# Moving a router's logits and prefixes from TensorE transposes to VectorE transposes in blocks of 32

The chip is a Trainium2; the kernel runs on one core. The metric is the device time of one execution in microseconds (us), lower is better.

## The reference, cut to what matters

A short causal convolution over 8 x 3584 tokens of 192 channels, then a mixture of experts: each token takes the expert of its largest logit, or the one of the token before it when a local gate says so.

```python
# conv: 7 taps, one set of weights for each of 8 heads of 24 channels
out = np.einsum('hk,bskhg->bshg', w, x_unf)
# router and experts: E = 8, D = 192, F = 1024
logits = np.einsum('bsd,de->bse', x, w_gate)
local_gate = 1.0 / (1.0 + np.exp(-np.einsum('bsd,de->bse', x, w_local).squeeze(-1)))
for b in range(B):
    prev_e = -1
    for s in range(S):
        fresh_e = int(np.argmax(logits[b, s]))
        if s == 0 or local_gate[b, s] < 0.5:
            e = fresh_e
        else:
            e = prev_e if prev_e >= 0 else fresh_e
        prev_e = e
        p = ...                     # softmax of logits[b, s]
        h = np.maximum(x[b, s] @ w1[e], 0.0)
        out[b, s] = p[e] * (h @ w2[e])
```

## The kernel before

Tokens come in 16 groups of 128 x 14. For each group VectorE, ScalarE and (for groups 0 and 1) TensorE do the convolution; the router finds each token's expert and its slot; GpSimd scatters the rows to their slots in DRAM; 144 expert blocks gather rows, multiply and scatter the results. The first 35 blocks hold one unit of 128 tokens, the next 87 two, the last 22 one. The router's logits need tokens' channels on partitions, so TensorE transposes them first:

```python
for u in range(3):                                   # three sets of 16 transposes
    tps = [hps_p.tile([P, 4 * GQ, DR], F32, name="hps") for half in range(2)]
    ...
                turn_half(tps[half][:, GQ * j + q, :], src, half)
    ...                                              # ScalarE evicts
lps = hps_p.tile([P, 2 * P], F32, name="hps")
for u in range(3):
    for j in range(4):                               # 12 products, 32 columns wide
        nc.tensor.matmul(lps[32 * j:32 * j + 32, :w], lhsT=wg[:, u, :],
                         rhs=yT[:, u, j, :w], start=(u == 0), stop=(u == 2))
# ... four transposes back; later two transposes for the carry, one back,
nc.tensor.matmul(nps[:, :E], lhsT=tri, rhs=mine, start=True, stop=True)    # prefix
nc.tensor.matmul(nps[:, E:2 * E], lhsT=ones, rhs=mine, start=True, stop=True)
```

The main loop deals out this work in steps between the products; `put()` issues one scatter of 128 routed rows:

```python
for i, (_, n, _, _) in enumerate(blocks):
    ensure(i)
    weights(i + AHEAD)
    hT = hidden(n, wbs[i], xT)
    if i + 1 < len(blocks):
        xT = turn(blocks[i + 1][1], xgs[i + 1])
    step(2.1 * n, 1)                      # conv and router work, then one put()
    output(n, wbs.pop(i), xgs.pop(i), hT)
    step(2.1 * n, n)                      # the same, then n put()
```

## Time and profile before

| | us |
|---|---|
| timed runs before the change (3) | 1482.4 to 1483.17, median 1482.96 |
| span of the execution that was profiled | 1412.9 |
| of which until block 0 / one-unit blocks / two-unit blocks / last 22 | 71.8 / 220.4 / 993.1 / 127.5 |

The stages run from the start of a block's first hidden product to that of a later one. Where TensorE does nothing but blocks, a two-unit block takes 10.81 us, so 87 would take 940.5. The first two lines don't agree by 70 us (68 by the profiled execution's own time, 1414.58).

### The profile page before, as it was taken

To read this page: it belongs to the slowest core of one execution; us is meant where nothing else is said; L and a number is where in the kernel's file an instruction comes from. 1 tells how busy PE (TensorE), PEld (TensorE's weight loads), DVE (VectorE), ACT (ScalarE), POOL (GpSimd) and SP (SyncE) were. 2 spreads that over 40 slices of the span, in tenths; PEclk is the share of its full clock that TensorE was granted. 3 is DMA by queue.
4 is the path that set the end of the run, shared out by engine and by line. 5 is a ranking of instruction groups with operands and counts; after the bars stand their busy time and mean duration, and the time that the engine had idled before them with its cause. 6 is when DMAs were issued, how large, how long until landed. Compare 5 with 4: busy or idle time off the path is not lost.

```text
span 1412.9 us, 41146 instructions
## 1 busy us (share of the span) xinstructions
PE 1377.8 (98%) x17132; PEld 1292.3 (91%) x17132; DVE 754.4 (53%) x1947; ACT 488.0 (35%) x1168; POOL 495.5 (35%) x524
## 2 busy tenths in 40 slices
PE   6788999999999999999999999999999999999998
PEld 4488999999999999999999999999999999999998
DVE  6767878777777777777777776241111111111111
ACT  3234344343333433334333343322222222222332
POOL 1342345344343443444434344344212111211111
PEclk9899999999999999999999999999999999999999
DMA  4399989977575775757757556566555555557893
GB/s 173 103 397 361 329 335 415 363 278 296 184 282 201 262 262 203 268 202 263 263 202 268 202 207 209 200 222 238 203 175 200 204 178 179 204 186 247 314 327 136
DMA packets 66476, 343.99 MB, mean 243 GB/s; under 512 B 12656, under 2 KB 23655, under 8 KB 45810
## 3 DMA queue, kind: packets, MB, share of 16 engines
q1 hardware_dynamic: 44064, 288.66, 56.6%
q0 software_dynamic: 22224, 52.70, 9.7%
q8 instruction: 135, 2.21, 0.6%
q14 instruction: 51, 0.42, 0.1%
q10 hardware_dynamic: 2, 0.00, 0.0%
HBM read 288.51 MB, written 53.49 MB: 242 GB/s over the span
## 4 chain that ended last, share of the span: by engine, by line
PE 62%; issue 27%; POOL 6%; DMA 3%; ACT 1%; DVE 1%; POOLq 0%; SPq 0%; ACTq 0%
PE yps L660 26%; PE hps L645 26%; POOL out_dram L674 5%; PE xps L264 2%; PE hps L264 2%; PE hps L308 2%; POOL slots L467 1%; DMA wb<-in_w_dram 1%; PE yps L185 1%; PE hps L185 1%; DMA xg<-slots 1%; DMA x_sb<-in_x_dram 1%; DMA out_dram<-o_sb,xg 0%; DVE y_sb L202 0%; PE hps L407 0%
## 5 line engine op out<-in xcount | busy, mean ns | idle before, releaser
L645 PE MATMUL hps<-xT,wb 64*128 64x256 f32 (+1 forms) x6912 | 635.1, 337 | 1.7 <-DMA wb<-in_w_dram 1.0
L660 PE MATMUL yps<-wb,hT 64*128 64x192 f32 x7392 | 635.8, 325 | 0.0
L645 PEld LDWEIGHTS hps<-xT,wb 64*128 64x128 f32 x6912 | 568.8, 188 | 45.3 <-DVE o_sb L670 5.4
L660 PEld LDWEIGHTS yps<-wb,hT 64*128 64x128 f32 x7392 | 601.1, 188 | 1.1 <-issue 0.9
L674 POOL DMA_INDIRECT out_dram<-o_sb,xg x231 | 236.9, 1025 | 772.4 <-DVE o_sb L670 681.7
L202 DVE SCALAR_TENSOR_TENSOR y_sb<-x_sb,c,y_sb 128x336 f32<-128x336 f32 x720 | 412.6, 583 | 22.3 <-ACT y_sb L177 6.6
L650 ACT ACTIVATE hT<-hps 128x512 f32<-128x512 f32 (+1 forms) x576 | 263.9, 510 | 379.9 <-PE hps L645 379.9
L467 POOL DMA_INDIRECT slots<-y_sb,posi x224 | 219.6, 980 | 115.4 <-issue 107.5
L669 ACT ACTIVATE o_sb<-yps,xg 128x192 f32<-128x192 f32 x231 | 87.6, 418 | 482.7 <-PE yps L660 482.7
L670 DVE SCALAR_TENSOR_TENSOR o_sb<-yps,xg,o_sb 128x192 f32<-128x192 f32 x231 | 88.3, 414 | 293.5 <-ACT o_sb L669 278.2
L625 DVE COPY xT<-xps 128x768 f32<-128x768 f32 x87 | 83.3, 957 | 236.1 <-PE xps L264 236.1
L264 PEld LDWEIGHTS xps<-ident,xg 64*128 64x128 f32 x1386 | 66.4, 140 | 13.6 <-issue 4.5
L264 PE MATMUL xps<-ident,xg 64*128 64x64 f32 x1386 | 67.8, 222 | 5.6 <-DMA xg<-slots 5.6
L628 DVE COPY xT<-xps 128x384 f32<-128x384 f32 x57 | 31.6, 555 | 70.4 <-PE xps L264 70.3
L177 ACT ACTIVATE y_sb<-x_sb,c 128x336 f32<-128x336 f32 x116 | 67.0, 589 | 0.4
L301 ACT COPY yT<-hps 128x512 f32<-128x512 f32 x93 | 49.8, 598 | 2.6 <-PE hps L264 2.2
L308 PE MATMUL hps<-yT,wg 128*32 128x256 f32 (+1 forms) x384 | 24.5, 358 | 2.7 <-issue 2.4
L264 PE MATMUL hps<-ident,y_sb 64*128 64x64 f32 x512 | 21.1, 223 | 2.8 <-DVE y_sb L202 1.7
L264 PEld LDWEIGHTS hps<-ident,y_sb 64*128 64x128 f32 x512 | 19.8, 139 | 4.2 <-ACT y_sb L177 1.8
L185 PE MATMUL hps<-x_sb,wb 128*128 128x336 f32 x56 | 18.7, 502 | 4.1 <-DMA x_sb<-in_x_dram 4.1
L308 PEld LDWEIGHTS hps<-yT,wg 128*32 128x32 f32 x384 | 11.9, 109 | 10.8 <-issue 5.7
L185 PEld LDWEIGHTS hps<-x_sb,wb 128*128 128x128 f32 x56 | 12.0, 217 | 10.5 <-issue 6.1
(142 smaller groups left out, 369.0 us busy)
## 6 DMA issues: line engine op xcount, KB each, us to landing
wb<-in_w_dram SPq DMA_DIRECT2D x144, 1536.0 KB
x_sb<-in_x_dram SPq DMA_DIRECT2D x16, 1920.0 KB
xg<-slots SPq DMA_DIRECT2D x87, 258.0 KB
xg<-slots SPq DMA_DIRECT2D x57, 129.0 KB
out_dram<-o_sb,xg POOLq DMA_INDIRECT x231
slots<-y_sb,posi POOLq DMA_INDIRECT x224
slots<-pad SPq DMA_DIRECT2D x1, 129.0 KB
slots<-pad,toi POOLq DMA_INDIRECT x8
```

The lines of the kernel that those rows point to most:

```text
L177: nc.scalar.activation(cols(h), chans(h, 0), Act.Copy, scale=c[:, h, 0:1])
L202: nc.vector.scalar_tensor_tensor(cols(h), chans(h, k), c[:, h, k:k + 1], cols(h), Alu.mult, Alu.add)
L264: nc.tensor.transpose(to, src[rows], identity=ident[rows, rows])
L308: nc.tensor.matmul(lps[32 * j:32 * j + 32, :w], lhsT=wg[:, u, :], rhs=yT[:, u, j, :w], start=(u == 0), stop=(u == 2))
L467: ins = nc.gpsimd.indirect_dma_start(out=slots[:, :], in_=rows, in_offset=None, out_offset=bass.IndirectOffsetOnAxis(ap=to, axis=0)).ins
L625: nc.vector.tensor_copy(to.rearrange("p h d k s -> p h (d k) s"), at.rearrange("p h d k s -> p h (d k) s"))
L645: nc.tensor.matmul(hps[half][:, j, w], lhsT=wb[rows, f0:f0 + P], rhs=xT[rows, d, w], start=(d == 0 and j == 0), stop=(d == KD - 1), skip_g ...
L650: nc.scalar.activation(hT[:, m:m + 2, w], hps[half][:, :, w], Act.Relu)
L660: nc.tensor.matmul(yps[half][:, k * D:(k + 1) * D], lhsT=hT[rows, m, k * P:(k + 1) * P], rhs=wb[rows, WA + m * D:WA + (m + 1) * D], start= ...
L669: nc.scalar.activation(o_sb[:, k, :], y[0], Act.Copy, scale=gate)
L670: nc.vector.scalar_tensor_tensor(o_sb[:, k, :], y[1], gate, o_sb[:, k, :], Alu.mult, Alu.add)
L674: sent = nc.gpsimd.indirect_dma_start(out=out, in_=o_sb[:, k, :], in_offset=None, out_offset=bass.IndirectOffsetOnAxis(ap=xg.bitcast(I32)[ ...
```

## The change

VectorE transposes the tokens where they lie, in blocks of 32 x 32 within a partition group of 32. The logits are then 48 small products (64 rows, 32 columns of weights, 128 tokens) in one visit to TensorE, eight side by side in the array. Carry and prefix over partitions go through VectorE's transposes and scans, not through TensorE. Groups 0 and 1 keep the old path. The diff, cut to its core (where weights are loaded and how the router's are laid out is left out):

```diff
+    def logits(g, y_sb):
+        ...
+        for t in range(0, NT, TQ):                        # TQ = 4 of 14 columns
+            nc.vector.transpose(z[:, t:u, :], y_sb[:, t:u, Y0:Y0 + D])
+        yield "hop"
+        lps = [hps_p.tile([P, TQ * Q], F32, name="hps") for half in range(2)]
+        begin = [min(TQ * j, NT - TQ) for j in range(4)]
+        for b in range(DQ):                               # DQ = 6 blocks of 32 channels
+            for j in range(4):
+                for half, rows in halves():
+                    nc.tensor.matmul(lps[half][Q * j:Q * j + Q, :], lhsT=wgq[rows, b, :],
+                                     rhs=z[rows, begin[j]:begin[j] + TQ, b * Q:(b + 1) * Q],
+                                     start=(b == 0), stop=(b == DQ - 1))
+        ...            # two ScalarE copies, a transpose back, 16 VectorE copies of 32 partitions
-        rps = hps_p.tile([P, GQ * P], F32, name="hps")
-        nc.tensor.transpose(rps[:1, :P], run[:, NT - 1:NT], identity=ident)
-        nc.tensor.transpose(rps[:1, P:2 * P], keep, identity=ident)
+            nc.vector.transpose(rT..., rk...)             # carry: 2 transposes, 10 small copies
-        nc.tensor.matmul(nps[:, :E], lhsT=tri, rhs=mine, start=True, stop=True)
-        nc.tensor.matmul(nps[:, E:2 * E], lhsT=ones, rhs=mine, start=True, stop=True)
+            nc.vector.transpose(mT, mk)                   # prefix: 2 transposes, 2 scans, 8 copies
-        step(2.1 * n, 1)
+        step(2.5 if n == 1 else 4.2, 1)
-        step(2.1 * n, n)
+        step(2.5 if n == 1 else 4.2, n)
```

## The prediction

> **What bounds the kernel now.** I read the page first, then the stretches by engine, the chain that ended last in order of time, and the timelines of TensorE and VectorE. The page's busy line:
>
> ```profile
> PE 1377.8 (98%) x17132; PEld 1292.3 (91%) x17132; DVE 754.4 (53%) x1947; ACT 488.0 (35%) x1168; POOL 495.5 (35%) x524
> ```
>
> TensorE is busy throughout, but an average hides stages, so I cut the span. Columns: stretch, length, busy time of PE, PEld, DVE, ACT, POOL with counts, granted clock, DMA share, GB/s.
>
> ```profile
> 125.00:180.00 55.00, 55.00 (x875) 53.35 (x874) 42.45 (x117) 23.59 (x67) 17.10 (x17) 1.00 0.95 357
> 410.00:470.00 60.00, 60.00 (x731) 55.23 (x729) 44.86 (x115) 23.26 (x54) 26.15 (x26) 1.00 0.67 242
> 925.00:1290.00 365.00, 365.00 (x4214) 353.25 (x4212) 63.99 (x145) 97.82 (x204) 85.10 (x88) 1.00 0.56 195
> ```
>
> There are three stages. From about 72 to 292 us the expert blocks hold one unit of 128 tokens, and TensorE, DMA (0.95) and VectorE are all nearly full. From 292 to about 925 us blocks hold two units; TensorE alone is full, VectorE at 75%, while conv and router of groups 5 to 15 run beside. After 925 us no routing is left. The routing groups are 2 to 15; groups 0 and 1 are routed in the prologue, on a path that the change keeps. What the router costs TensorE is seen in the chain of the middle stage (start, length, piece):
>
> ```profile
> 351.61 0.50 PE hps L264 x16
> 357.71 0.50 PE hps L264 x16
> 358.22 5.25 PE yps L660 x64
> 363.47 1.43 PE hps L308 x15
> 364.90 5.38 PE hps L645 x48
> 376.03 0.20 PE hps L362
> 376.23 0.11 PE hps L363
> 382.09 0.15 PE hps L376
> 387.64 0.32 PE hps L407 x2
> 387.96 0.22 PE hps L408 x2
> 399.19 5.18 PE hps L645 x44
> ...
> 417.10 2.98 PE yps L660 x35
> ```
>
> The reader is to see that the router's pieces stand between blocks of hidden (L645) and output (L660) products with no gap: each is time on the path. One group repeats after 417.10 - 358.22 = 58.88 us and holds five blocks. A block without routing is read from the timeline of TensorE after 925 us:
>
> ```profile
> 1010.15 5.43 PE L660 MATMUL yps<-wb,hT 64*128 64x192 f32 x64
> 1020.95 5.43 PE L660 MATMUL yps<-wb,hT 64*128 64x192 f32 x64
> ```
>
> 10.80 us, so five are 54.0, and a group's routing costs 4.9 us of TensorE. By pieces: three sets of 16 transposes 1.5, logits 1.43, four transposes back 0.12, carry 0.31 + 0.15, prefix 0.54, together 4.05; the other 0.8 is in the pieces that follow an interruption (5.38 against 5.18).
>
> In the first stage it is VectorE that I distrust. Its timeline over one conv-only block:
>
> ```profile
> 168.75 0.55 DVE L628 COPY xT<-xps 128x384 f32<-128x384 f32 x1
> 169.22 2.37 DVE L202 SCALAR_TENSOR_TENSOR y_sb<-x_sb,c,y_sb 128x336 f32<-128x336 f32 x4
> 171.65 0.42 DVE L670 SCALAR_TENSOR_TENSOR o_sb<-yps,xg,o_sb 128x192 f32<-128x192 f32 x1
> 171.98 2.26 DVE L202 SCALAR_TENSOR_TENSOR y_sb<-x_sb,c,y_sb 128x336 f32<-128x336 f32 x4
> 174.17 0.55 DVE L628 COPY xT<-xps 128x384 f32<-128x384 f32 x1
> ```
>
> Eight taps (about 0.58 us each) and two evictions take 5.42 us without a gap, and TensorE's one-unit block takes 5.52. VectorE is already even with TensorE here.
>
> **What the Trainium skill says.** "TensorE: Matmul & The Clock Gate", Part 3: products of at most 64 rows or 32 columns run side by side in different tiles, each further tile starting some 4 ns later. The trace agrees on columns: the 12 logits products (9 of 256 columns, 3 of 128, 2688 in all) took 1.43 us; at the 0.437 us per lone 256-column product (24 hidden products, two abreast, in 5.24) they would take 4.6, so over three ran at once. "TensorEngine Tiling (Array Packing)", Key Properties: changing the tiling mode drains the array; the 0.2 us after a visit fits. "Vector Engine (DVE) Microarchitecture Reference", 3.8: the 32x32 transpose sustains one element per cycle per lane; no such operation is in this trace. "VectorE: DVE Perf Modes", Two Vector instructions with no wait between them: an instruction whose start quadrant differs from the last one's waits for all earlier ones. The small copies added here go from quadrant to quadrant; the trace before has none such.
>
> **The change, part by part.** I compared the built programs. For 14 groups TensorE loses 48 + 4 transposes, 12 wide logits products, two carry transposes, one back and two prefix products; it gains 48 products of 64 rows x 32 columns x 128 tokens, in one visit.
> - The visit: 24 one-unit hidden products of 128 columns, two abreast, take 2.68 us, 0.223 a round. Eight abreast, 48 products are 6 rounds: 1.34 us, with a start and the slower piece after it some 1.7. If issue limits instead, the closest measured rate is 16 transposes in 0.50 us, 31 ns for a load and a product; 48 products are 96 such pairs (two records each): 3.0, with its surroundings 3.2. I take 1.9, nearer the first, because four tiles abreast are shown and eight are not.
> - Gain on the path in the middle stage: 4.9 - 1.9 = 3.0 a group. Eleven groups: 33 us.
> - VectorE gains per group 2688 transposed columns in four pieces (an estimate of 0.96 GHz by the skill's clock: 2.8 + 0.3), one of 256 columns (0.35), four small ones, and some 34 small copies. Copies of this size take 0.13 to 0.17 here; overlapped they add 0.09, held 0.16. Sum 8 to 10 us. ScalarE loses six evictions of 0.60, two of lsb, two of lt and three small ones, and gains two copies of 0.25: off the path.
> - In the middle stage the built order gives six blocks a group, not five, with 55 to 57 us of VectorE in 6 x 10.8 + 1.9 = 66.7 us. It fits. Routing ends some ten blocks later, still ahead of need.
> - In the first stage the budget per step goes from 2.1 to 2.5: conv-only blocks hold ten taps, 0.47 + 0.33 + 10 x 0.58 = 6.6 us, over TensorE's 5.52. Adding VectorE's pieces over blocks 1 to 34 in the built order gives 202 to 209 us, against 173 before; TensorE needs 34 x 5.52 + 3 x 1.9 = 193, and the stage took 220 before with its DMA waits. The three groups' TensorE gain (9 us) is thus mostly taken back by VectorE: I count 0, from -8 to +8.
> - Prologue: a shorter copy, five more memsets, a larger weight load: under 1 us. After 925 us: nothing.
>
> Sum: 33 us off. The profiled run took 1414.58, the timed ones 1483; I cannot explain the 68 us from this trace and take the saving as it is: 1450.
>
> **The rivals.**
> (a) The visit is limited by issue, not streaming. For: nothing here shows pairs closer than 31 ns. Against: those transposes load 128 columns each, and loads of 32 should be shorter (L308's mean load is 109 ns, the transposes' 139). It would leave 1.7 a group: 19 us, 1464, within 2%.
> (b) VectorE becomes the bound of the first stage and costs more than TensorE gains. For: the 6.6 us blocks. Against: the lighter blocks between (4.8 to 5.7) and some 2 us of slack from the output products let it average. At worst 10 us lost: 1460.
> (c) The logits visit waits for VectorE's transposes, a new wait in place of those removed. Against: the order puts the visit a step after them, and hidden plus output products give 5 us of slack in the middle stage. If it happened, 1 us a group: 1461.
> (d) All router TensorE time was hidden anyway. The chain contradicts it: it ran through these pieces, and the period was 4.9 longer than the same blocks without.
>
> **Range and chances.** Streaming (60%) gives 34 to 39 off, issue-bound 19 to 25; the first stage adds 8 either way; if the timed runs are slower all through, the gain grows by 5%. That spans 1434 to 1466. The 2% line is 29.7 us off, 1453.3: a little above my centre. Faster by over 2%: 0.6; within 2%: 0.38; slower: 0.02.
>
> **What would show it.** Right: the logits visit takes 1.4 to 1.9 us in the chain; two-unit groups repeat every 66 to 67 us with six blocks; VectorE's busy time grows by about 110 to 140 us; the first two-unit block starts within 8 us of 292. Wrong: a visit near 3 us (rival a); the chain of the first stage running through VectorE with the stage longer than 220 us (b); TensorE idle just before the visit, released by VectorE (c).

## The result, and the profile after

1476.59 us median (1474.74 to 1480.2, 4 runs) against 1482.77 (1482.4 to 1483.17, 4 runs): ratio 0.9961, 95% interval 0.9942 to 0.998, so within 2%. A ratio here is the mean time of one kernel's fast runs over that of the other's of the same rounds, so not quite the ratio of the medians quoted. A time is compared only with one of the same chip.

The busy line of the page after (busy us, share of the span, instructions):

```profile
PE 1393.4 (94%) x17314; PEld 1315.6 (89%) x17314; DVE 896.7 (61%) x2605; ACT 434.6 (29%) x1014; POOL 479.3 (33%) x515
```

TensorE is at 94%, where the profile before had 98%: it has become idle in places, and VectorE has grown by 142 us, just over the 110 to 140 foreseen. The chain in order of time through one logits visit (start, length, piece):

```profile
529.09 0.59 PE hps L350 x31
529.67 0.17 issue
...
531.73 0.32 issue
532.04 1.07 PE hps L350 x50
533.11 5.40 PE yps L756 x64
```

L350 is the line of the 48 products (96 records). The visit takes 533.11 - 529.09 = 4.0 us instead of the predicted 1.9. Its first 31 records and its last 50 run at about 20 ns each; between them TensorE stands still several times, and the profile calls that "issue": it waited for nothing that is recorded. Such stops stand in the output products too. So the first question was whether the profile before, which has hardly any, is of a usual execution.

### The profile page after: what moved, and what is told of

It reads as the page before. It is cut to its first block, busy times and chain, and to the rows that moved or that the text cites. A ratio compares the mean times of both kernels' runs of the same rounds, so it can differ in the third digit from the quotient of the medians.

```text
span 1474.5 us, 41949 instructions
## 1 busy us (share of the span) xinstructions
PE 1393.4 (94%) x17314; PEld 1315.6 (89%) x17314; DVE 896.7 (61%) x2605; ACT 434.6 (29%) x1014; POOL 479.3 (33%) x515
## 4 chain that ended last, share of the span: by engine, by line
PE 58%; issue 23%; DVE 8%; POOL 5%; DMA 2%; another core or an unknown queue 2%; ACT 1%; POOLq 0%; DVEq 0%; SPq 0%; ACTq 0%
PE yps L756 26%; PE hps L741 24%; POOL out_dram L770 4%; DVE y_sb L206 3%; PE hps L350 3%; PE xps L278 2%; POOL slots L566 1%; PE yps L189 1%; PE hps L189 1%; DMA wb<-in_w_dram 1%; DVE xT L727 1%; DVE o_sb L766 1%; DMA out_dram<-o_sb,xg 1%; DMA x_sb<-in_x_dram 0%
## 5 line engine op out<-in xcount | busy, mean ns | idle before, releaser
L756 PE MATMUL yps<-wb,hT 64*128 64x192 f32 x7392 | 672.4, 327 | 23.2 <-issue 19.1
L756 PEld LDWEIGHTS yps<-wb,hT 64*128 64x128 f32 x7392 | 615.3, 188 | 48.4 <-issue 42.7
L741 PEld LDWEIGHTS hps<-xT,wb 64*128 64x128 f32 x6912 | 608.6, 188 | 21.8 <-DVE xT L727 9.5
L206 DVE SCALAR_TENSOR_TENSOR y_sb<-x_sb,c,y_sb 128x336 f32<-128x336 f32 x720 | 402.9, 568 | 20.3 <-ACT y_sb L181 2.5
L278 PEld LDWEIGHTS xps<-ident,xg 64*128 64x128 f32 x1386 | 78.0, 140 | 3.4 <-PE hps L741 0.3
L278 PE MATMUL xps<-ident,xg 64*128 64x64 f32 x1386 | 77.0, 223 | 0.1
L350 PE MATMUL hps<-z,wg 64*32 64x128 f32 x1344 | 44.7, 286 | 16.0 <-issue 15.7
L350 PEld LDWEIGHTS hps<-z,wg 64*32 64x32 f32 x1344 | 25.5, 110 | 32.0 <-issue 31.1
L366 DVE COPY lt<-lq 32x36 f32<-32x36 f32 x224 | 44.6, 199 | 3.3
L340 DVE STREAM_TRANSPOSE z<-y_sb 128x768 f32<-128x768 f32 (+1 forms) x56 | 44.1, 844 | 0.0
```

Source lines behind the costliest of these rows:

```text
L206: nc.vector.scalar_tensor_tensor(cols(h), chans(h, k), c[:, h, k:k + 1], cols(h), Alu.mult, Alu.add)
L278: nc.tensor.transpose(to, src[rows], identity=ident[rows, rows])
L350: nc.tensor.matmul(lps[half][Q * j:Q * j + Q, :], lhsT=wgq[rows, b, :], rhs=z[rows, begin[j]:begin[j] + TQ, b * Q:(b + 1) * Q], start=(b = ...
L741: nc.tensor.matmul(hps[half][:, j, w], lhsT=wb[rows, f0:f0 + P], rhs=xT[rows, d, w], start=(d == 0 and j == 0), stop=(d == KD - 1), skip_g ...
L756: nc.tensor.matmul(yps[half][:, k * D:(k + 1) * D], lhsT=hT[rows, m, k * P:(k + 1) * P], rhs=wb[rows, WA + m * D:WA + (m + 1) * D], start= ...
```

## The experiments

"Gap" below means: two weight loads of TensorE start over 0.4 us apart, counted in the trace of the two-unit stage from 330 to 1340 us, from start to start. So it holds the usual step from load to load too (0.08 us in output products, 64 in 5.4), and sums of gaps are somewhat more than the time lost.

### The kernel before again, the budget, and the size of the visit (chip 5)

`e1_before` is the kernel before, unchanged.

> The kernel before, unchanged, for a new profile: its timed runs are 1483 us, but the profile on which the prediction rests was of an execution of 1414.6, while the changed kernel's profile (1476.3) agrees with its timed runs. Theory U (the profile of before was of a lucky execution; the timed ones lose some 68 us in a way it does not show): the new profile is near 1481 us, with gaps of TensorE that are put down to issue, as the changed kernel's profile shows them. Rival (the profiler itself makes this kernel faster): the profile is again near 1413 us with no such gaps, the timed runs near 1483. Time against before: 1.00.

Measured: 1481.88 us, ratio 0.9997 (0.998 to 1.0013); profiled span 1483.9. From its page, and its view of what TensorE waited for (us in total, times, longest):

```profile
PE 1416.5 (95%) x17132; PEld 1326.4 (89%) x17132; DVE 742.9 (50%) x1947; ACT 493.8 (33%) x1168; POOL 493.8 (33%) x524
PE yps L660 <- issue: 15.1, 34, 1.1
```

The same program at 95% of 1483.9 us, not 98% of 1412.9: on this chip it has the gaps as well, 60 us of them in the two-unit stage, where the first profile had 18. Theory U held: that profile was of another kind of execution than the timed runs.

`e2_budget` gives the steps of the changed kernel back their old budget.

```diff
-        step(2.5 if n == 1 else 4.2, 1)
+        step(2.1 * n, 1)
-        step(2.5 if n == 1 else 4.2, n)
+        step(2.1 * n, n)
```

> The changed kernel with the old step budget (2.1 per one-unit step instead of 2.5). Theory V (VectorE is the bound of the first stage because conv-only blocks hold ten taps): the first two-unit block starts earlier than the 321 us of the changed kernel, near 300, and the time falls by 10 to 25 us, to about 1455. Rival S (TensorE's instruction supply costs the time, stage by stage, whatever VectorE does): the first stage shortens by less than 5 us and the time is within 0.5% of the changed kernel's 1476.

Measured: 1488.15 us, 1.0048 (1.0029 to 1.0068). Its one-unit stage is shorter (217.1 us against 240.4) and its two-unit stage longer (1057.2 against 1025.5): less routing is done early and more late. The first two-unit block does start at 297.7 us, as theory V said, but the time rises by 12 us instead of falling; S, which had the first stage almost unchanged, missed too. The new budget isn't what ate the gain.

`e3_half` uses two column tiles of 224 columns, so 24 products instead of 48; `e4_few` does only the first 8 of the 48, with a wrong result.

```diff
-TQ = (NT + 3) // 4                  # e3_half
+TQ = (NT + 1) // 2
-            for j in range(4):
+            for j in range(2):
-        for b in range(DQ):         # e4_few
+        for b in range(1):
```

> The logits visit of the changed kernel as 24 products of 7 tokens x 32 instead of 48 of 4 x 32: two column tiles instead of four, four abreast instead of eight. Half the instructions (48 load and product pairs instead of 96), longer streaming: 6 rounds x 224 columns, an estimate of 2.3 us from the 0.223 us a round of 128 columns takes. Theory S (the visit is limited by the supply of instructions to TensorE: in the changed kernel's profile it takes 4.0 us with gaps of 0.3 us after every 4 or 5 records): the visit falls from 4.0 to 2.4 to 3.0 us, and the time by 11 x 1 to 1.5 = 11 to 17 us, to about 1462. Rival (streaming or the tile-mode switch limits the visit): it gets longer, 4.5 us or more, and the time rises by 5 us or more. Eight copies and two long transposes on VectorE instead of sixteen and four also take 1.6 us a group off VectorE.

> Wrong result on purpose: the logits visit does only the first 8 of its 48 products; all else is as in the changed kernel (the numbers of blocks do not depend on the routing). It measures what the visit costs in all. Theory S: the gaps put down to issue in and near the visits go with the 40 products, a group repeats some 4 us sooner, and the time falls by 14 x 3 to 4 = 42 to 56 us, to about 1425. Rival (the gaps are not the visit's; they come at every so many instructions anyway): the visit's 4 us go but gaps appear in the products that follow, and the time falls by less than 25 us.

Measured: 1455.16 us, 0.9816 (0.9799 to 0.9833), and 1433.0, 0.9666 (0.965 to 0.9682). Fewer products in the visit do gain. The visits of `e3_half` in the two-unit stage take 3.1 to 3.8 us, above theory S's 2.4 to 3.0 and below its rival's 4.5, and the time fell further than S said. `e4_few` gains 44 us on the changed kernel, inside S's 42 to 56. But with 8 products left there are still 52 us of gaps, mostly inside output products, so the visit is not their only place.

### The parts alone, and work added at the end (chip 1)

After the last group is routed some 25 two-unit blocks run undisturbed; `f1_busy` and `f2_visits` add one suspected cost there. `pa_logits` has the new logits with the old carry and prefix on TensorE, `pb_prefix` the reverse.

```diff
         # pa_logits: carry and prefix as before, by transposes and products of TensorE
-        if alone:                       # carry
+        if not alone:
+            rps = hps_p.tile([P, 2 * P], F32, name="hps")
+            nc.tensor.transpose(rps[:1, :P], run[:, NT - 1:NT], identity=ident)
         ...
-        if alone:                       # prefix: TensorE's branch for all groups
+        if True:
         # pb_prefix
-        lt = yield from (wide_logits if alone else logits)(g, y_sb)
+        lt = yield from wide_logits(g, y_sb, alone)
         # f1_busy, each step of a two-unit block at the end
+        for _ in range(6):
+            nc.vector.scalar_tensor_tensor(toy[:, 0, :], toy[:, 1, :], c[:, 0, 0:1],
+                                           toy[:, 0, :], Alu.mult, Alu.add)
+        ...                                  # two ScalarE copies, one GpSimd copy
         # f2_visits, every sixth step there: the 48 products on a constant tile
```

> The new logits alone (VectorE transposes, one visit), with carry and prefix through TensorE as in the kernel before. Theory S (the visit is held up by TensorE's supply of instructions, about 4.0 us where the old pieces took 1.5 + 1.43 + 0.12 = 3.05): this part gains nothing, about 1.0 us a group lost for 11 to 14 groups, less what the longer group period saves; about 1487 us, from 1479 to 1495, visit 3.6 to 6 us in the chain. Rival (the visit is well paid for, and the gain of the change comes from it): 1476 or less.

> The new carry and prefix on VectorE alone, with the old transposes and wide logits products on TensorE. It takes five short pieces, 0.31 + 0.15 + 0.54 = 1.0 us a group, from TensorE and adds no burst. Theory S: this part carries the gain, 11 to 16 us: about 1469 us (1464 to 1475), faster than the whole change. Rival (the visit carries it): 1480 or more.

> The changed kernel; after the last group is routed, each of the two steps of a two-unit block adds idle work of about the size that conv and router have: six VectorE operations of 128x336, two ScalarE copies, one GpSimd copy, with nothing that waits for them. TensorE's program and all transfers stay. Rival O (TensorE's gaps in the middle stage come of the other engines' work, which delays what its products wait for): the undisturbed blocks grow from 10.81 us to 11.3 to 11.6, some 25 of them, 1488 to 1497 us. Theory S: they stay at 10.81, time as the changed kernel, 1475 to 1479.

> The changed kernel; after the last group is routed, every third two-unit block gets a further visit of 48 of the same products on a constant tile, with no conv, router or VectorE work beside it. Theory S: the visit is slow by itself where it meets the edge of a fetched piece of the program, 2.5 to 4.5 us each as in the middle stage, and the blocks around it show gaps too: some 8 visits, +24 to +36 us, about 1505. Rival O: without other work beside it a visit takes its streaming time with a restart, 1.4 to 1.7 us, and no gaps appear: +12 to +15 us, about 1490.

Measured: 1405.6, 1397.46, 1381.9 and 1395.64 us. The kernel before stood at 1412.95 (1412.04 to 1416.15, 7 runs), not at 1482: this chip gives the time of the first profile. The ratios are 0.994 (0.9923 to 0.9956), 0.9886 (0.987 to 0.9903), 0.978 (0.9763 to 0.9796) and 0.9871 (0.9854 to 0.9887). The absolute times expected were worked out for 1482 and don't apply, and nor does a test of gaps where there are none. What stands: both parts gain, 7.3 and 15.5 us (in the two-unit stage 18.6 and 19.7; the one-unit stage of `pa_logits` is 10 us longer, 230.7); the idle work of `f1_busy` costs nothing, its blocks staying at 10.81 us; and eight visits added in `f2_visits` cost 1.7 us each (13.4 us of records for them in the groups of its profile).

`g1_after` is the changed kernel unaltered, `g2_half` the same as `e3_half`, both on chip 1.

> The changed kernel itself, unaltered, to be read with the time of the kernel before in the same call, because the last call stood at 1413 us for the kernel before where the earlier ones stood at 1482. Theory C (the prediction's steps hold where TensorE gets its instructions in time, and the gain is lost only where it doesn't): if the kernel before stands near 1413, the changed one takes 1376 to 1384, ratio 0.974 to 0.980, visit 1.6 to 1.75 us; if it stands near 1482, about 1476 again, ratio 0.994 to 0.998. Rival (the idle work of f1_busy and the added visits of f2_visits changed something else, and the changed kernel gains little anywhere): ratio above 0.985 in both.

> The visit with two column tiles of 224 columns instead of four of 128: 24 products instead of 48, the same as e3_half. Theory C: near 1413 for the kernel before, the visit takes 24 products at two tiles of rows by two of columns, four abreast, 6 rounds of 224 columns: 6 x 0.39 = 2.3 us with its restart, 0.6 to 0.7 more than the 1.7 of four column tiles, so 7 to 10 us more than the changed kernel: 1384 to 1392. Near 1482 for the kernel before: 1455 again. So the better form would hang on the supply. Rival: it is faster than the changed kernel in both, as fewer instructions are better anywhere.

Measured: 1381.6 us (1380.91 to 1382.89), ratio 0.9774 (0.9758 to 0.979), and 1389.45, 0.983 (0.9813 to 0.9846). What theory C said of a chip of 1413 came true in all of it; what it said of one of 1482, and its reason, were not tested here. The busy line and the chain of `g1_after`:

```profile
PE 1342.8 (97%) x17314; PEld 1273.7 (92%) x17314; DVE 896.5 (65%) x2605; ACT 434.2 (31%) x1014; POOL 484.5 (35%) x515
```

```profile
554.15 1.67 PE hps L350 x94
555.82 5.40 PE yps L756 x64
...
620.81 1.72 PE hps L350 x94
```

The visit takes 1.7 us without a stop, and the next one comes 66.66 us later, six blocks of 10.81 and the visit. Here the change gains 31 us. With 24 products the visit takes 2.40 us (six rounds of 224 columns instead of 128), and is the slower form.

### Whether it is the visit or other engines' work (chips 12, 10)

`h1_phases` puts three stretches into the end of one kernel: visits, plain blocks, and idle work of other engines. `h2_third` uses three column tiles of 160 columns, 36 products.

```diff
+            steps[0] += 1                    # h1_phases, after the last group is routed
+            if steps[0] <= 16:
+                if steps[0] % 4 == 0:
+                    visit()
+            elif steps[0] > 32:
+                busy()
-TQ = (NT + 3) // 4                           # h2_third
+TQ = (NT + 2) // 3
```

> The changed kernel; after the last group is routed, the two-unit blocks come in three stretches: eight with a visit of 48 products in every second one, eight as they are, the rest with idle VectorE, ScalarE and GpSimd work of the size of conv and router. It is for a chip on which the kernel before takes about 1482 us; on one of 1413 it only repeats what f1_busy and f2_visits showed (about 1389 us, visits 1.65 us, no gaps). At 1482: theory V (a visit alone runs TensorE's supply dry) has the four visits at 2.5 to 4.5 us with gaps in the outputs near them, and the last stretch at 10.81 us a block. Theory O (all engines draw on one slow supply, so TensorE starves only where the others fetch too) has visits of 1.6 to 2 us, no gaps in the first two stretches, and 11.3 to 11.6 us a block in the last one.

> Three column tiles of 160 columns: 36 products where the change has 48 and the half form 24, six abreast. Per round 160 columns at the rate of the half form (2.40 us for 6 rounds of 224 columns, 0.40 a round): 6 x 0.286 = 1.7 us, the same as the visit of 48 (1.70), so with 24 fewer of its 96 pairs at no loss. At 1413 for the kernel before: 1381 to 1384, ratio 0.976 to 0.980. At 1482: between the change (1476) and the half form (1455), about 1465.

Measured on chip 12, where the kernel before took 1413.24: 1390.85 us (2 runs) and 1381.69, 0.9779 (0.9762 to 0.9795). A visit of 36 products takes 1.78 us, so its fewer records are no gain and no loss there. The four added visits of `h1_phases` take 1.83, 1.84, 1.83 and 1.52 us; the difference is taken up below. To get to a slow chip both were sent again, unaltered, as `h3_phases` and `h4_third`.

> The same kernel as h1_phases, sent again in the hope of a chip on which the kernel before takes about 1482 us, where alone it can tell the theories apart. There, theory V (a visit alone runs TensorE's supply dry): four visits of 2.5 to 4.5 us with gaps in the outputs near them, the last stretch at 10.81 us a block. Theory O (all engines draw on one slow supply): visits of 1.6 to 2 us, no gaps in the first two stretches, 11.3 to 11.6 us a block in the last. On a chip of 1413 it repeats h1_phases, 1389 to 1393 us, and tells nothing new.

> The same kernel as h2_third, to see the form of 36 products at 1482 for the kernel before: about 1465, between the change (1476) and the half form (1455), if the loss goes with the number of TensorE instructions; 1474 or more if it goes with the number of visits or of blocks in a group. On a chip of 1413: 1381 to 1383 again.

This came to chip 10, where the kernel before took 1502.35 (1500.9 to 1504.28). Measured: 1513.11 us (2 runs), and 1494.97, 0.9948 (0.9932 to 0.9965): 36 products gain no more than 48 did, against what was expected, so the loss doesn't go simply with the count of TensorE instructions. Its visits in the two-unit stage take 4.1 to 4.4 us; why the 24 products of `e3_half` lost less stays open.

`h3_phases` refuted both theories. Against O: in its last stretch, where VectorE is busy for 53.5 of 68 us with idle work, the blocks follow each other every 10.81 us. Against V: three of its visits are slow and the fourth isn't. The chain at the first and at the fourth (L864 is the visit), with the timeline of GpSimd at each:

```profile
1122.54 0.56 PE hps L864 x22
1123.10 0.77 issue
1123.88 0.39 PE hps L864 x3
1124.27 1.05 issue
1125.32 1.82 PE hps L864 x61
```

```profile
1118.13 0.98 POOL L770 DMA_INDIRECT out_dram<-o_sb,xg  x1 [6.51 <-DVE o_sb L766]
1119.41 0.98 POOL L770 DMA_INDIRECT out_dram<-o_sb,xg  x1 [0.30 <-issue]
1120.70 0.96 POOL L566 DMA_INDIRECT slots<-y_sb,posi  x1 [0.31 <-issue]
1121.97 0.96 POOL L566 DMA_INDIRECT slots<-y_sb,posi  x1 [0.30 <-issue]
1123.23 0.96 POOL L566 DMA_INDIRECT slots<-y_sb,posi  x1 [0.30 <-issue]
```

```profile
1204.59 1.52 PE hps L864 x96
1206.11 5.40 PE yps L756 x64
```

```profile
1200.09 0.98 POOL L770 DMA_INDIRECT out_dram<-o_sb,xg  x1 [7.27 <-DVE o_sb L766]
1201.38 0.98 POOL L770 DMA_INDIRECT out_dram<-o_sb,xg  x1 [0.30 <-issue]
```

At the first visit GpSimd is at the end of five scatters in a row: two of results, three of routed rows. The stops begin 1.0 to 1.1 us after the start of the fourth and of the fifth. At the fourth visit only the two scatters of results run, and it takes 1.52 us on the same chip. `h1_phases`, the same kernel on chip 12, shows the same order on a small scale: scatters run in fives up to its first three visits (1.83 us), and only the two of results before the fourth (1.52). So on a chip of 1413 the scatters cost a visit 0.3 us, and here some 3. After the last scatter into the slots (1191.86) there is no further gap up to 1340 us. So I sorted all gaps by the scatter that started last, within 2.5 us before them. A run is of scatters that start less than 1.9 us apart; the entries are gaps in us behind a scatter of that place in its run:

| trace | chip's time of the kernel before | 1st | 2nd | 3rd | 4th | 5th | no scatter near |
|---|---|---|---|---|---|---|---|
| before, first profile | about 1413 (by its span) | 0 | 0 | 0 | 0 | 0 | 17.6 |
| e1_before | 1482 | 0 | 0 | 0 | 11.8 | 28.7 | 19.7 |
| changed kernel | 1483 | 0.6 | 12.1 | 13.6 | 12.2 | 35.4 | 0 |
| e4_few | 1482 | 0 | 0.7 | 2.6 | 13.8 | 35.5 | 0 |
| g1_after | 1413 | 0 | 0 | 0 | 0 | 0 | 0 |

The gaps with no scatter near, in the two traces of the kernel before, stand at the edges of the router's old pieces, all but one of them 0.41 or 0.52 us long, on both kinds of chip. The gaps behind a 2nd and 3rd scatter in the changed kernel are those of the visit, where a GpSimd copy of the wrapped columns parts a run of five in the count. The changed kernel had 74 us of gaps behind scatters (26 in ten visits, 48 in output products), the kernel before 40.

### The runs of scatters taken apart (chips 12, 8)

That was a coincidence in time, still. `i1_spread` (the changed kernel) and `i2_spread_before` (the kernel before, with its own budget) make GpSimd wait for the hidden products before it scatters routed rows, so that no more than three scatters follow each other. Nothing of TensorE's program changes; GpSimd gets one small copy a block, which does the waiting.

```diff
-        step(2.5 if n == 1 else 4.2, 1)
+        step(2.5 if n == 1 else 4.2, 1 if n == 1 else 0)
+        if n == 2 and to_put:
+            nc.gpsimd.tensor_copy(mark, hT[:, FK - 1, 0:1])
+            for _ in range(3):
+                put()
         output(n, wbs.pop(i), xgs.pop(i), hT)
-        step(2.5 if n == 1 else 4.2, n)
+        step(2.5 if n == 1 else 4.2, 1 if n == 1 else 0)
```

> The changed kernel with GpSimd's scatters taken apart in the two-unit blocks: the three scatters of routed rows wait for the hidden products and stand before the output products, so that no more than three scatters follow one another; the same scatters in number, TensorE's program the same. Theory G (on a chip of 1482 to 1502 us for the kernel before, TensorE's gaps are set off by runs of four or five scatters): the gaps behind scatters, 74 us of the changed kernel's two-unit stage, fall to under 20; the visit takes 1.7 to 2 us; 1405 to 1430 us. Rival (the scatters only happen to stand there; the supply is slow by itself): gaps and time within 10 us of the changed kernel's, 1470 or more. On a chip of 1413 both say 1380 to 1386.

> The kernel before with the same scatters taken apart in the same way. Theory G, on a chip of 1482 to 1502 for the kernel before: it loses its 40 us of gaps behind runs of scatters, about 1440 to 1455, and the changed kernel with the same edit is faster than it by what the prediction said, 2.0 to 2.5%. Rival: within 10 us of the kernel before. On a chip of 1413: 1411 to 1417.

They came to chip 12, the kernel before at 1412.8: 1380.71 us, 0.9775 (0.9757 to 0.9792), and 1412.48, 1.0001 (0.9983 to 1.0018). As both theories said there: no gain, and no cost of the edit. Again, as `j1_spread` and `j2_spread_bef`:

> The same kernel as i1_spread, sent again in the hope of a chip on which the kernel before takes 1482 us or more; on one of 1413 it tells nothing new (1379 to 1383). Where the kernel before takes 1482 to 1502, theory G (runs of four or five scatters set off TensorE's gaps): gaps behind scatters in the two-unit stage under 20 us instead of 74, visits of 1.7 to 2 us, 0.95 to 0.965 of the time of the kernel before, where the changed kernel was 0.996. Rival (the scatters only happen to stand there): 0.99 or more.

> The kernel before with the runs of scatters taken apart, the same as i2_spread_before, sent again in the hope of a slow chip. There the changed kernel with this edit took 0.9452 of the kernel before. Theory G: this one takes 0.965 to 0.975, so that the change alone, both with the edit, is worth 2 to 2.5% as on the other chips. Rival (the edit helps only the changed kernel's visit): 0.985 or more. On a chip of 1413: 1411 to 1415 again.

Both came to chip 8, the kernel before at 1502 (1499.5 to 1504.9, 8 runs). Measured: 1421.48 us (1416.8 to 1425.53), ratio 0.9452 (0.9424 to 0.9479), and 1447.1 (1446.33 to 1451.4), 0.9642 (0.9619 to 0.9665). The chain and the timeline of GpSimd at a visit of `j1_spread` (L896 is the added wait):

```profile
443.02 5.25 PE yps L756 x63
...
453.83 1.52 PE hps L350 x96
```

```profile
443.77 0.18 POOL L896 COPY mark<-hT 128x1 f32<-128x1 f32 x1 [1.96 <-ACT hT L746]
444.46 0.98 POOL L566 DMA_INDIRECT slots<-y_sb,posi  x1 [0.51 <-issue]
445.75 0.96 POOL L566 DMA_INDIRECT slots<-y_sb,posi  x1 [0.30 <-issue]
447.01 0.96 POOL L566 DMA_INDIRECT slots<-y_sb,posi  x1 [0.30 <-issue]
450.07 0.98 POOL L770 DMA_INDIRECT out_dram<-o_sb,xg  x1 [2.10 <-DVE o_sb L766]
```

Three scatters, a pause of 2 us, then two: the visit is whole again, and 13 us of gaps are left in the two-unit stage (17 behind scatters in `j2_spread_bef`). The three scatters fall into output products, which take their 5.25 us all the same, which speaks for the length of the run and not for its place. Only the time and order of GpSimd's scatters were touched, so on the slow chips the runs do cause the gaps. The visits came out shorter than expected (1.52 us in nine of ten), and both ratios lie just below the ranges given (0.95 and 0.965). With the edit in both kernels, the change is worth 0.9452 / 0.9642 = 0.980 there (25.6 us by the medians), at the edge of the 2 to 2.5% expected. The changed kernel without the edit was not run on chip 8.

The two-unit stage (87 blocks, us) sums it up. In the second row the first two kernels ran at 1482 (`e1_before` on chip 5, and the result), the other two on chip 8, at 1502, so its columns compare in pairs only:

| | kernel before | changed | before, scatters apart | changed, scatters apart |
|---|---|---|---|---|
| chips at 1413 | 993.1 | 958.9 | 993.1 | 957.9 |
| chips at 1482 (left pair), 1502 (right pair) | 1033.4 | 1025.5 | 994.1 | 968.5 |

The changed kernel with the scatters apart is level with the changed kernel on chips of 1413 (1380.7 against 1381.6 us) and the fastest on the slow ones for its chip (1421.5).

## Why the prediction was wrong, point by point

- The visit, 1.9 us with 1.4 to 1.9 as the sign: right on the chips of 1413, 1.67 to 1.73 us in the two-unit stage of `g1_after`, and 1.52 with the scatters apart. The 48 products do run eight abreast: six rounds at the prediction's 0.223 us make 1.34, twelve would make 2.68. In the profile after it took 4.1 to 5.0 us in the two-unit stage and up to 5.7 before it. Rival (a), limited by issue, has the right name but the wrong cause: the records of an undisturbed visit follow at 18 ns, well under the 31 ns it assumed.
- Gain in the two-unit stage, 3.0 us for eleven groups, 33 in all: 34.2 us on the chip of 1413 (993.1 to 958.9), 25.6 on the slow chip with the scatters apart, but 7.9 at 1482 as they are (1033.4 to 1025.5). The period of 66 to 67 us with six blocks: 66.7 in `g1_after`, 72.1 to 73.3 in the profile after.
- First stage, 0 within 8: 222.6 against 220.4 on the chip of 1413, 240.4 against 242.2 at 1482. The first two-unit block at 293.9 in `g1_after`, within 8 us of 292, but at 321.1 in the profile after, where the kernel before has 322.5 (`e1_before`): the sign failed by the chip, not by the change. Rival (b) didn't decide. The prediction's "nearly full" is too much for VectorE in this stage: its own line has 42.45 of 55 us, 77%, hardly more than the 75% of the two-unit stage. VectorE's growth of 110 to 140 us: 142, slightly over, since the 16 small copies take 0.20 us each and don't overlap.
- Rivals (c) and (d) are out: no stop before a visit is put down to VectorE, and `g1_after` gains what the pieces on the path were worth.
- The step that failed is the last one of the sum: "I cannot explain the 68 us from this trace and take the saving as it is." The 68 us were not a constant that both kernels would carry. In good part (40 of some 70) they were gaps of TensorE behind runs of four or five GpSimd scatters, on a kind of chip that the profile of before doesn't show, and the change alters how much these cost. In the kernel before they hit long output products: its two-unit stage is 40.3 us longer on such a chip. In the changed kernel they hit the visit as well, where 96 records should pass in 1.7 us: its stage is 66.6 us longer. The 26.3 us more (ten visits of 4.2 instead of 1.8 us are 24 of them) come off the 34.2 that were to be gained and leave 7.9. The range put 5% on the gain for slower runs where it needed a second case, almost no gain. Its upper end is also less than its own terms make: 19 off by issue and 8 back in the first stage are 1472, not 1466; the 1476.6 measured lies beyond both.

What stays open: why some chips behave so (5, 8 and 10) and others hardly (1, 12), and by which way a scatter holds up TensorE. TensorE's supply of instructions is a guess. The Trainium skill, "Runtime: NRT & Kernel Launch", Instruction fetch mechanics, has the program refilled in blocks of 256 instructions by a DMA queue of the sequencer's own and calls the cost mostly hidden. The traces show these transfers, 16 KB each, one in about 11 us, but they take 0.96 to 0.99 us in the median on both kinds of chip, and of the changed kernel's 107 gaps only 23 overlap one, so nothing here shows that TensorE waits for them. The 13 to 25 us by which a kernel's one-unit stage is longer on the slow chips, and the 9 to 11 us until block 0, were not taken away by any run; the edit of `j1_spread` leaves one-unit blocks as they are.

## What to carry to other kernels

When a profile's span and the timed runs differ by more than the change is to gain, profile the unchanged kernel again on the chip that is timed before anything is read from it: a bound or a saving read from the other kind of execution can be right and still not appear. Idle time that waits for nothing can come from an engine that shares no data with the idle one, so set its times beside the other engines' timelines before explaining it by the idle engine's own program. On such a chip a dense burst of short instructions lost most (a visit of 1.8 us took 4.2), so keep GpSimd's scatters out of long runs, above all beside it.

## What the Trainium skill lacked or had wrong

- No page has it: the same kernel takes 1413 us on some chips and 1482 to 1502 on others, at nearly the same granted clock (kernel before: 0.989 to 0.994 against 0.983 to 0.989). A time is only to be compared with one of the same chip.
- No page has it, and it would belong to "Runtime: NRT & Kernel Launch": on the slow chips two weight loads of TensorE start 0.4 to 1.4 us apart within 1.4 us of the start of a GpSimd scatter of 128 rows that is mostly the fourth or fifth in a row, 74 us in the two-unit stage of the changed kernel; no more than three in a row leave 13. On a chip of 1413 such runs lengthen a visit from 1.52 to 1.83 us.
- "TensorE: Matmul & The Clock Gate", Part 3, agrees on small tiles side by side. It gives the span of one pack of tiles, a product and some 4 ns for each further tile, not of several packs in a row: 48 fp32 products of 64 rows x 32 columns took 1.7 us at 128 columns, eight abreast; 36 of 160 columns, six abreast, 1.78; 24 of 224 columns, four abreast, 2.40.
- "VectorE: DVE Perf Modes", Two Vector instructions with no wait between them, agrees: copies from quadrant to quadrant don't overlap. The 168 of 32 x 36 elements in `g1_after` were busy for 32.8 us, 0.195 us each, which is their mean length.
- "Vector Engine (DVE) Microarchitecture Reference", 3.8, agrees: transposes of 128 x 768 elements took 0.95 us on average, and a group's 2688 columns 3.2, where one element per cycle, at the 0.96 GHz that the prediction took, made an estimate of 2.8, and with its 0.3 for the starts 3.1.
